# Longer rows for q, k and the weights, and an earlier first block, in a fused attention and feed-forward kernel

## The chip, the cores and the metric

One core of one Trainium2 chip. The metric is the time of one execution on the device, in microseconds; lower is better. The kernel before takes 399.72 us (median of 3 runs, 399.69 to 401.94). A profiled execution's span, from first to last instruction, is about 2 us shorter than its time.

## The reference, cut to what matters

```python
# q, k, v: (8 batches, 8 heads, 576 positions, 64), s: (8, 8, 576)
scores = q @ k.T / 8
cum = cumsum(max(s, 0))                       # a decay along the sequence
bias = min(-(cum[query] - cum[key]), 0)       # causal positions only
attn = softmax(where(causal, -1e9, scores + bias))
x = (attn @ v)        # -> (4608 tokens, 512)
h = x @ w_in          # 512 -> 2048
g = h * clip(h + 3, 0, 6) / 6
return g @ w_out      # 2048 -> 512
```

The kernel works on 32 pairs of heads (four pairs are a batch of 576 tokens) and nine blocks of 512 tokens. "Layer 1" of a block is h and g, "layer 2" is the product with w_out.

## The kernel before: the parts that the argument touches

Loads of a pair, with `NTR` = 9 tiles of 128 rows. Every contiguous piece is one row of 64 fp32 numbers, 256 bytes:

```python
    def load_qk(p, eng):
        t = work.tile([128, NTR, 2, D], F32, tag="qkf", bufs=3, name=f"qkf{p}")
        for i, src in enumerate((q, k)):
            eng.dma_start(
                out=t[:, :, i, :],
                in_=src[b, h0:h0 + 2].rearrange("h s d -> (h s) d").rearrange(
                    "(t p) d -> p t d", p=128
                ),
            )
```

The cast to fp16 on GpSimd (`cast_qk`) is followed by transposes on TensorE into PSUM, in two groups of five and four tiles, and by copies out of PSUM, one for q (rows 0 to 63) and one for k (64 to 127):

```python
        nc.vector.tensor_copy(out=qT[0:64, sl, c0:c0 + n], in_=pT[0:64, 0:n])
        nc.vector.tensor_copy(out=kT[0:64, sl, c0:c0 + n], in_=pT[64:128, 0:n])
```

Four more rows of kT and qT carry the decay (`kaug`, `qaug`). They are computed once for all heads with the heads on partitions, stored to DRAM, and read back for each pair. The last lines weave the work: attention of batch 0 alone, layer 1 of block 0 beside batch 1, then both layers of consecutive blocks beside a batch each:

```python
    weave(att_of[1], m1_tasks(0))
    for n in range(NBLK - 1):
        att = att_of[n + 2] if n + 2 < B else []
        weave(att, merged(m1_tasks(n + 1), m2_tasks(n)))
```

PSUM is full: two banks "M" (layer 1, early transposes), three "S" (scores), two "O" (attend), one "Y" (layer 2).

The softmax here doesn't subtract the row's maximum and nothing guards it: scores larger than these inputs give would overflow.

## Time and profile before

| kernel before | |
|---|---|
| time, median | 399.7 us |
| span of the profile | 397.3 us |
| first exponential | 16.4 us |
| layer 1 of block 0 starts | 45.0 us |
| layer 1 of block 1 starts ("the landmark") | 85.1 us |
| from one block's start to the next, later | 40.1 us |
| last matmul ends | 393.2 us |

The first 80 us are bound by DMA and the rest by TensorE; the prediction below shows the lines that say so. A group's row reads: line, engine, operation, what it writes and reads, count; busy time and mean duration; idle time of the engine before it and what ended most of that. In the kernel before, the copies out of the transposes are these (groups by form):

```profile
L181 DVE COPY qT<-pT 64x640 f16<-64x640 f16 x32 | 15.2, 476 | 16.4 <-PE pT L171 16.4
L182 DVE COPY kT<-pT 64x640 f16<-64x640 f16 x32 | 15.8, 493 | 0.4
L182 DVE COPY kT<-pT 64x512 f16<-64x512 f16 x32 | 13.6, 426 | 0.4
L181 DVE COPY qT<-pT 64x512 f16<-64x512 f16 x32 | 13.1, 408 | 1.3 <-PE pT L171 1.3
```

About 0.45 us each, 57.7 us of DVE for all 32 pairs, on an engine that is busy for 57% of the span.

### The profile page before, as it was taken

How to read it: one execution, taken by the hardware profiler on the slowest of the kernel's cores; microseconds unless marked ns; L12 is line 12 of the kernel's file. 1: busy time of each engine (PE TensorE's matmuls, PEld its weight loads, DVE VectorE, ACT ScalarE, POOL GpSimd, SP SyncE). 2: the span in 40 equal slices, each digit the busy share in tenths (PEclk: the TensorE clock that was granted, in tenths of full speed). 3: DMA queues.
4: the chain of work that ended last, by engine and by line, in shares of the span. 5: the costliest groups of instructions: out<-in, count | busy, mean ns of one | idle time of the engine just before them, and what ended most of it. 6: DMA issues, size and time to landing. Idle time of an engine off the chain costs nothing.

```text
span 397.3 us, 8194 instructions
## 1 busy us (share of the span) xinstructions
PE 366.4 (92%) x3040; PEld 209.7 (53%) x3040; DVE 227.2 (57%) x417; ACT 210.8 (53%) x406; POOL 140.3 (35%) x333
## 2 busy tenths in 40 slices
PE   7584776899999999999999999999999999999985
PEld 3363443555555555555555555555555544444432
DVE  4574372756666666666666666666665564454511
ACT  6364473755555566666666555555556633443400
POOL 3394825544444444444444444444443200000000
PEclk9999698999999999999999999999999999999999
DMA  9999999955555555554555455455100001010111
GB/s 176 201 213 205 185 208 178 194 108 118 116 118 118 119 117 118 119 117 117 118 118 118 108 126 114 109 126 116 38 28 27 28 26 54 26 53 28 49 58 54
DMA packets 123512, 43.40 MB, mean 109 GB/s; under 512 B 114192, under 2 KB 118672, under 8 KB 123472
## 3 DMA queue, kind: packets, MB, share of 16 engines
q1 hardware_dynamic: 117456, 37.89, 43.9%
q0 software_dynamic: 4224, 4.19, 6.4%
q10 hardware_dynamic: 1792, 0.79, 0.9%
q8 instruction: 24, 0.39, 0.4%
q14 instruction: 16, 0.13, 0.1%
HBM read 37.32 MB, written 9.73 MB: 118 GB/s over the span
## 4 chain that ended last, share of the span: by engine, by line
PE 80%; DMA 10%; POOL 4%; DVE 3%; ACT 2%; issue 1%; SPq 0%; POOLq 0%; ACTq 0%
PE po L335 31%; PE ph L317 29%; PE S L211 8%; DMA qkf<-in_k_dram 7%; PE O L260 6%; PE pT L171 3%; PE pX L285 2%; POOL Pm L224 2%; POOL t L153 1%; DMA kaug_scratch<-kaug 1%; DMA kT<-kaug_scratch 1%; ACT trl L325 1%; ACT Pm L219 1%; DMA s_sb<-in_s_dram 1%; DVE osb L344 1%; DVE gT L326 1%
## 5 line engine op out<-in xcount | busy, mean ns | idle before, releaser
L326 DVE SCALAR_TENSOR_TENSOR gT<-trl,ph 128x512 f16<-128x512 f32 x144 | 98.8, 687 | 114.7 <-ACT trl L325 114.5
L219 ACT ACTIVATE Pm<-S 128x384 f16<-128x384 f32 (+2 forms) x256 | 113.7, 506 | 80.3 <-PE S L211 72.5
L317 PE MATMUL ph<-xT,w_in_sb 128*128 128x512 f16 x576 | 147.4, 381 | 0.0
L335 PE MATMUL po<-w_out_sb,gT 128*128 128x512 f16 x576 | 144.4, 379 | 2.3 <-DVE osb L344 2.3
L325 ACT ACTIVATE trl<-ph,bias 128x512 f32<-128x512 f32 x144 | 99.6, 692 | 82.8 <-PE ph L317 81.0
L224 POOL TENSOR_SCALAR_AFFINE_SELECT Pm<-Pm 128x128 f16<-128x128 f16 (+2 forms) x256 | 78.8, 313 | 154.6 <-ACT Pm L219 144.8
L211 PE MATMUL S<-qT,kT 128*128 128x320 f16 (+4 forms) x448 | 71.4, 265 | 8.0 <-DMA kT<-kaug_scratch 3.0
L335 PEld LDWEIGHTS <-gT 128*128 128x128 f16 x576 | 51.2, 98 | 49.4 <-issue 3.2
L317 PEld LDWEIGHTS <-w_in_sb 128*128 128x128 f16 x576 | 52.2, 98 | 44.5 <-issue 1.1
L211 PEld LDWEIGHTS <-kT 128*128 128x128 f16 x448 | 42.1, 99 | 35.3 <-issue 4.9
L153 POOL CAST t<-qkf 128x1152 f16<-128x1152 f32 x32 | 36.7, 1147 | 21.4 <-DMA qkf<-in_k_dram 21.4
L260 PEld LDWEIGHTS <-Pm 128*128 128x128 f16 x960 | 37.4, 97 | 7.8 <-POOL Pm L224 1.6
L260 PE MATMUL O<-v_h,Pm 128*128 128x65 f16 x960 | 40.8, 193 | 0.5 <-POOL Pm L224 0.5
L171 PE MATMUL pT<-ident,t 128*128 128x128 f16 x288 | 26.8, 222 | 13.5 <-POOL t L153 12.9
L181 DVE COPY qT<-pT 64x640 f16<-64x640 f16 x64 | 28.3, 442 | 17.7 <-PE pT L171 17.6
L171 PEld LDWEIGHTS <-t 128*128 128x128 f16 x288 | 21.1, 99 | 28.1 <-POOL t L153 14.6
L344 DVE TENSOR_SCALAR osb<-po 128x512 f32<-128x512 f32 x36 | 24.8, 690 | 13.8 <-PE po L335 13.2
L182 DVE COPY kT<-pT 64x640 f16<-64x640 f16 x64 | 29.4, 459 | 0.9
L272 DVE TENSOR_TENSOR xs<-O,r 128x640 f16<-128x640 f32 x32 | 26.4, 824 | 1.1
L159 POOL CAST v_h<-v_f 128x640 f16<-128x640 f32 x28 | 20.1, 718 | 0.0
L285 PEld LDWEIGHTS <-xs 128*128 128x128 f16 x160 | 11.8, 99 | 10.9 <-issue 6.2
L293 DVE COPY xT<-pX 128x576 f16<-128x576 f16 x32 | 14.5, 453 | 1.7 <-PE pX L285 1.5
(29 smaller groups left out, 56.6 us busy)
## 6 DMA issues: line engine op xcount, KB each, us to landing
qkf<-in_q_dram SPq DMA_DIRECT2D x32, 288.0 KB
qkf<-in_k_dram SPq DMA_DIRECT2D x32, 288.0 KB
out_dram<-osb SPq DMA_DIRECT2D x36, 256.0 KB
v_f<-in_v_dram SPq DMA_DIRECT2D x62, 128.0 KB
w_in_sb<-in_moe_w_in_dram POOLq DMA_DIRECT2D x4, 512.0 KB, 8.1
w_out_sb<-in_moe_w_out_dram POOLq DMA_DIRECT2D x4, 512.0 KB, 10.1
v_f<-in_v_dram SPq DMA_DIRECT2D x31, 32.0 KB
kT<-kaug_scratch SPq DMA_DIRECT2D x30, 6.8 KB
```

Of the source, the lines that this page charges most:

```text
L153: nc.gpsimd.tensor_copy(out=t, in_=qk_f.pop(p))
L171: nc.tensor.matmul(out=pT[:, (t - t0) * 128:(t - t0 + 1) * 128], lhsT=src[:, t, :, :], rhs=ident, is_transpose=True, start=(t == t0), stop ...
L182: nc.vector.tensor_copy(out=kT[0:64, sl, c0:c0 + n], in_=pT[64:128, 0:n])
L211: nc.tensor.matmul(out=S[:, c:c + hi - lo], lhsT=kT[:, sl, off + 128 * kt:off + 128 * (kt + 1)], rhs=qT[:, sl, off + lo:off + hi], start=( ...
L219: nc.scalar.activation(out=P[:, p0:p0 + n], in_=S[:, 0:n], func=AF.Exp, scale=0.125, bias=0.0)
L224: nc.gpsimd.affine_select(out=view, in_=view, pattern=pattern, compare_op=ALU.is_ge, fill=0.0, base=0, channel_multiplier=-1,)
L260: nc.tensor.matmul(out=O[:, hh, qt * VW:qt * VW + D + 1], lhsT=P[:, c:c + 128], rhs=v_h[:, sl, hh, kt, 0:D + 1], start=(qt == 0), stop=(qt ...
L317: nc.tensor.matmul(out=ph, lhsT=w_in_sb[:, kc, f * 128:(f + 1) * 128], rhs=xT[:, kc, n * 512:(n + 1) * 512], start=(kc == 0), stop=(kc == ...
L325: nc.scalar.activation(out=trl, in_=ph, func=AF.Relu, bias=bias3[:, 0:1], scale=1.0)
L326: nc.vector.scalar_tensor_tensor(out=gT[n][:, f, :], in0=trl, scalar=6.0, in1=ph, op0=ALU.min, op1=ALU.mult)
L335: nc.tensor.matmul(out=po, lhsT=gT[n][:, f, t4 * 128:(t4 + 1) * 128], rhs=w_out_sb[:, f, :], start=(f == 0), stop=(f == NF - 1),)
L344: nc.vector.tensor_scalar_mul(out=osb, in0=po, scalar1=1.0 / 6.0)
```

## The change

The intent is to shorten the DMA-bound stage. For pairs 0 to 7 each partition reads nine consecutive rows of q and of k, 2304 bytes in one piece; the transposes then come out with neighbouring rows in different tiles, and the copies out of PSUM put them back in order. The weights are read in 8 KB rows, so that layer 1 takes every sixteenth column of w_in. The decay rows of pair 0 go from SBUF to SBUF. Casts of v move from DVE to ScalarE (pairs 1 to 4), casts of q and k move later, and layer 1 and half of layer 2 of block 0 stand beside batch 1. Three output tiles take an "M" bank. Smaller moves are cut from the diff below: the weight loads are issued one pair earlier, the transposes of the next pair stand ahead of an attend, and the warm-up matmuls are 18 and 12 instead of 22 and 10.

```diff
     def load_qk(p, eng):
...
+            rows = src[b, h0:h0 + 2].rearrange("h s d -> (h s) d")
+            if by_partition(p):                     # p < 8
+                eng.dma_start(
+                    out=t.rearrange("p (i t d) -> p i t d", i=2, d=D)[:, i],
+                    in_=rows.rearrange("(p t) d -> p t d", t=NTR),
+                )
...
     def cast_v(p):
-        eng = nc.vector if p in (1, 2, 3, 4) else nc.gpsimd
-        eng.tensor_copy(out=v_h[:, sl, :, :, 0:D], in_=v_f[:, sl])
+        copy = nc.scalar.copy if p in (1, 2, 3, 4) else nc.gpsimd.tensor_copy
+        copy(out=v_h[:, sl, :, :, 0:D], in_=v_f[:, sl])
...
-        nc.vector.tensor_copy(out=qT[0:64, sl, c0:c0 + n], in_=pT[0:64, 0:n])
-        nc.vector.tensor_copy(out=kT[0:64, sl, c0:c0 + n], in_=pT[64:128, 0:n])
+        for dst, r0 in ((qT, 0), (kT, 64)):
+            if by_partition(p):
+                nc.vector.tensor_copy(
+                    out=dst[0:64, sl, 0:W2].rearrange("d (p t) -> d t p", t=NTR)[:, t0:t1],
+                    in_=pT[r0:r0 + 64, 0:n].rearrange("d (t p) -> d t p", p=128),
+                )
...
     def load_w_in(c):
         nc.gpsimd.dma_start(
-            out=w_in_sb[:, :, c * 512:(c + 1) * 512],
-            in_=moe_w_in[:, c * 512:(c + 1) * 512].rearrange("(kc p) f -> p kc f", p=128),
+            out=w_in_sb[:, c, :], in_=moe_w_in[c * 128:(c + 1) * 128, :]
         )
     def load_w_out(c):
-            in_=moe_w_out[c * 512:(c + 1) * 512, :].rearrange("(ft p) j -> p ft j", p=128),
+            in_=moe_w_out.rearrange("(p f) j -> p f j", f=NF)[:, c * 4:(c + 1) * 4, :],
+    w_in_t = w_in_sb.rearrange("p k (m f) -> p k f m", f=NF)
...
-                lhsT=w_in_sb[:, kc, f * 128:(f + 1) * 128],
+                lhsT=w_in_t[:, kc, f, :],
...
+    load_qk(0, nc.sync)
+    load_qk(1, nc.sync)
+    mask_rows(0, nc.scalar.copy)
+    nc.scalar.activation(out=qaug, in_=c8, func=AF.Copy, scale=-1.0)
+    for hh in range(2):
+        nc.sync.dma_start(out=kT[64:65, 0, c0:c1], in_=kaug[hh:hh + 1, 0, :])
+        nc.scalar.dma_start(out=qT[67:68, 0, c0:c1], in_=qaug[hh:hh + 1, :])
+    for hh in range(2):
+        nc.sync.dma_start(out=kT[65:66, 0, c0:c1], in_=kaug[hh:hh + 1, 1, :])
+        nc.scalar.dma_start(out=kT[66:67, 0, c0:c1], in_=kaug[hh:hh + 1, 2, :])
+    load_v(0, nc.sync)
+    nc.sync.dma_start(out=kaug_dram..., in_=kaug)
+    nc.sync.dma_start(out=qaug_dram..., in_=qaug)
...
-    weave(att_of[1], m1_tasks(0))
+    weave(att_of[1], first + m2_0[:8])              # first: layer 1 of block 0
+    weave(att_of[2], merged(m1_tasks(1), m2_0[8:], 2))
```

More of the change, by code (lines that the diff above doesn't have):

```diff
@@ L118, with by_partition @@
     qk_h = {}
+    def by_partition(p):
+        return p < 8
     def load_qk(p, eng):
         b, h0 = (2 * p) // H, (2 * p) % H
-        t = work.tile([128, NTR, 2, D], F32, tag="qkf", bufs=3, name=f"qkf{p}")
+        t = work.tile([128, NTR * 2 * D], F32, tag="qkf", bufs=3, name=f"qkf{p}")
         for i, src in enumerate((q, k)):
-            eng.dma_start(
-                out=t[:, :, i, :],
-                in_=src[b, h0:h0 + 2].rearrange("h s d -> (h s) d").rearrange(
-                    "(t p) d -> p t d", p=128
-                ),
-            )
+            rows = src[b, h0:h0 + 2].rearrange("h s d -> (h s) d")
[4 more added lines that the diff above has]
+                )
+            else:
+                eng.dma_start(
+                    out=t.rearrange("p (t i d) -> p t i d", i=2, d=D)[:, :, i, :],
+                    in_=rows.rearrange("(t p) d -> p t d", p=128),
+                )
         qk_f[p] = t
@@ L152, in cast_qk @@
         t = work.tile([128, NTR, 2, D], F16, tag="qkh", bufs=2)
-        nc.gpsimd.tensor_copy(out=t, in_=qk_f.pop(p))
+        f = qk_f.pop(p)
+        if by_partition(p):
+            nc.gpsimd.tensor_copy(
+                out=t.rearrange("p t i d -> p i t d"),
+                in_=f.rearrange("p (i t d) -> p i t d", i=2, d=D),
+            )
+        else:
+            nc.gpsimd.tensor_copy(
+                out=t, in_=f.rearrange("p (t i d) -> p t i d", i=2, d=D)
+            )
         qk_h[p] = t
@@ L180, in transpose_group @@
         c0 = t0 * 128
-        nc.vector.tensor_copy(out=qT[0:64, sl, c0:c0 + n], in_=pT[0:64, 0:n])
-        nc.vector.tensor_copy(out=kT[0:64, sl, c0:c0 + n], in_=pT[64:128, 0:n])
+        for dst, r0 in ((qT, 0), (kT, 64)):
+            if by_partition(p):
+                nc.vector.tensor_copy(
+                    out=dst[0:64, sl, 0:W2].rearrange("d (p t) -> d t p", t=NTR)[:, t0:t1],
+                    in_=pT[r0:r0 + 64, 0:n].rearrange("d (t p) -> d t p", p=128),
+                )
+            else:
+                nc.vector.tensor_copy(out=dst[0:64, sl, c0:c0 + n], in_=pT[r0:r0 + 64, 0:n])
         if g == 1:
@@ L331, in m2 @@
         if part == 0:
-            pouts[n, t4] = psum.tile([128, 512], F32, tag="Y", bufs=1, name=f"po{n}_{t4}")
+            tag, bufs = ("M", 2) if (n, t4) in ((0, 1), (8, 1), (8, 3)) else ("Y", 1)
+            pouts[n, t4] = psum.tile([128, 512], F32, tag=tag, bufs=bufs, name=f"po{n}_{t4}")
         po = pouts[n, t4]
@@ L349 @@
     nc.vector.memset(bias3, 3.0)
-    load_qk(0, nc.sync)
-    load_v(0, nc.scalar)
-    load_qk(1, nc.sync)
-    load_v(1, nc.sync)
-    load_qk(2, nc.sync)
-    load_v(2, nc.sync)
-    mask_rows(0, nc.scalar.copy)
-    nc.scalar.activation(out=qaug, in_=c8, func=AF.Copy, scale=-1.0)
-    mask_rows(1, nc.scalar.copy)
-    nc.scalar.dma_start(
-        out=kaug_dram.rearrange("r (h t) -> h r t", h=NH), in_=kaug
-    )
-    nc.scalar.dma_start(out=qaug_dram.rearrange("r (h t) -> h (r t)", h=NH), in_=qaug)
-    load_aug(0, nc.scalar)
-    load_aug(1, nc.scalar)
     def keep_warm(n):
@@ L374, in keep_warm @@
             )
-    weights = {
-        1: [(load_w_in, 0)],
-        2: [(load_w_in, 1), (load_w_in, 2)],
-        3: [(load_w_in, 3)],
-        4: [(load_w_out, 0), (load_w_out, 1)],
-        5: [(load_w_out, 2), (load_w_out, 3)],
+    load_qk(0, nc.sync)
[3 more added lines that the diff above has]
+    for hh in range(2):
+        c0, c1 = hh * SEQ, (hh + 1) * SEQ
+        nc.sync.dma_start(out=kT[64:65, 0, c0:c1], in_=kaug[hh:hh + 1, 0, :])
+        nc.scalar.dma_start(out=qT[67:68, 0, c0:c1], in_=qaug[hh:hh + 1, :])
+    for hh in range(2):
+        c0, c1 = hh * SEQ, (hh + 1) * SEQ
+        nc.sync.dma_start(out=kT[65:66, 0, c0:c1], in_=kaug[hh:hh + 1, 1, :])
+        nc.scalar.dma_start(out=kT[66:67, 0, c0:c1], in_=kaug[hh:hh + 1, 2, :])
+    load_v(0, nc.sync)
+    nc.sync.dma_start(
+        out=kaug_dram.rearrange("r (h t) -> h r t", h=NH), in_=kaug
+    )
+    nc.sync.dma_start(out=qaug_dram.rearrange("r (h t) -> h (r t)", h=NH), in_=qaug)
+    mask_rows(1, nc.scalar.copy)
+    load_v(1, nc.sync)
+    load_qk(2, nc.sync)
+    load_aug(1, nc.sync)
+    load_v(2, nc.sync)
+    weights_at = {
+        0: [(load_w_in, 0)],
+        1: [(load_w_in, 1), (load_w_in, 2)],
+        2: [(load_w_in, 3)],
+        3: [(load_w_out, 0), (load_w_out, 1)],
+        4: [(load_w_out, 2), (load_w_out, 3)],
     }
     def att_tasks(p):
+        more = p + 1 < NP
         def loads():
@@ L392, in loads @@
                 load_v(p + 3, nc.sync)
-            for load, c in weights.get(p, []):
-                load(c)
-        more = p + 1 < NP
-        tasks = [(loads, 0)]
-        for bi in range(4):
-            tasks.append((lambda bi=bi: scores_bank(2 * p, bi), 400))
-        if p > 0:
-            tasks.append((lambda: attend(2 * p - 1), 1200))
-        if more:
-            tasks.append((lambda: transpose_group(p + 1, 0), 640))
-        for bi in range(4):
-            tasks.append((lambda bi=bi: scores_bank(2 * p + 1, bi), 400))
+            if p >= 4 and more:
+                cast_qk(p + 1)
         def casts():
@@ L409, in casts @@
                 cast_v(p + 1)
-            if p + 2 < NP:
+            if p + 2 <= 4:
                 cast_qk(p + 2)
-        tasks.append((casts, 0))
+            for load, c in weights_at.get(p, []):
+                load(c)
+        a = [(loads, 0)]
+        for bi in range(4):
+            a.append((lambda bi=bi: scores_bank(2 * p, bi), 400))
+        if more:
+            a.append((lambda: transpose_group(p + 1, 0), 640))
         if p > 0:
-            tasks.append((lambda: x_transpose(p - 1), 640))
+            a.append((lambda: attend(2 * p - 1), 1200))
+        for bi in range(4):
+            a.append((lambda bi=bi: scores_bank(2 * p + 1, bi), 400))
+        a.append((casts, 0))
         if more:
-            tasks.append((lambda: transpose_group(p + 1, 1), 512))
-        tasks.append((lambda: attend(2 * p), 1200))
-        return tasks
+            a.append((lambda: transpose_group(p + 1, 1), 512))
+        if p > 0:
+            a.append((lambda: x_transpose(p - 1), 640))
+        return a, [(lambda: attend(2 * p), 1200)]
+    att_of = [[]]
+    for p in range(NP):
+        a, c = att_tasks(p)
+        att_of[-1] += a
+        if p % 4 == 0 and p > 0:
+            att_of.append([])
+        att_of[-1] += c
+    att_of[-1] += [(lambda: attend(NH - 1), 1200), (lambda: x_transpose(NP - 1), 640)]
     def weave(att, mlp):
         total = float(sum(c for _, c in att)) or 1.0
-        done = 0.0
-        for i, task in enumerate(mlp):
-            while att and done / total < i / len(mlp):
+        whole = float(sum(w for _, w in mlp))
+        done, due = 0.0, 0.0
+        for task, w in mlp:
+            while att and done / total < due / whole:
                 a, c = att.pop(0)
@@ L430, in weave @@
             task()
+            due += w
         for a, c in att:
@@ L434, in m1_tasks, with merged @@
     def m1_tasks(n):
-        return [lambda f=f: m1(n, f) for f in range(NF)]
+        return [(lambda f=f: m1(n, f), 1.0) for f in range(NF)]
     def m2_tasks(n):
-        return [lambda t4=t4, part=part: m2(n, t4, part) for t4 in range(4) for part in range(4)]
-    def merged(a, b):
-        out_ = []
-        for t in range(4):
-            f, g = a[4 * t:4 * t + 4], b[4 * t:4 * t + 4]
-            out_ += [g[0], g[1], f[0], g[2], f[1], g[3], f[2], f[3]]
+        return [
+            (lambda t4=t4, part=part: m2(n, t4, part), 1.0)
+            for t4 in range(4) for part in range(4)
+        ]
+    def merged(a, b, rounds):
+        out_ = []
+        na = len(a) // rounds
+        for t in range(rounds):
+            f, g = a[na * t:na * (t + 1)], b[4 * t:4 * t + 4]
+            if na == 4:
+                out_ += [g[0], g[1], f[0], g[2], f[1], g[3], f[2], f[3]]
+            else:
+                out_ += [g[0], f[0], f[1], g[1], f[2], f[3], g[2], f[4], g[3]] + f[5:]
         return out_
-    keep_warm(22)
+    keep_warm(18)
     cast_qk(0)
@@ L454 @@
     cast_qk(1)
-    keep_warm(10)
-    att_all = []
-    cut = []
-    for b in range(B):
-        for p in range(4 * b, 4 * b + 4):
-            att_all += att_tasks(p)
-            if p % 4 == 0:
-                cut.append(len(att_all) - 2)
-    att_all += [(lambda: attend(NH - 1), 1200), (lambda: x_transpose(NP - 1), 640)]
-    cut.append(len(att_all))
-    att_of = [att_all[cut[b]:cut[b + 1]] for b in range(B)]
-    for task, _ in att_all[:cut[1]]:
-        task()
-    weave(att_of[1], m1_tasks(0))
-    for n in range(NBLK - 1):
-        att = att_of[n + 2] if n + 2 < B else []
-        weave(att, merged(m1_tasks(n + 1), m2_tasks(n)))
-    for task in m2_tasks(NBLK - 1):
+    keep_warm(12)
+    for task, _ in att_of[0]:
+        task()
+    first = m1_tasks(0)
+    first = [(task, 0.3) for task, _ in first[:8]] + [(task, 0.6) for task, _ in first[8:]]
+    m2_0 = m2_tasks(0)
+    weave(att_of[1], first + m2_0[:8])
+    weave(att_of[2], merged(m1_tasks(1), m2_0[8:], 2))
+    for n in range(2, NBLK):
+        weave(
+            att_of[n + 1] if n + 1 < B else [], merged(m1_tasks(n), m2_tasks(n - 1), 4)
+        )
+    for task, _ in m2_tasks(NBLK - 1):
         task()
```

## The prediction

> **What bounds the kernel now.** I read the slices of the page first, to see where the span is not full.
>
> ```profile
> PE   7584776899999999999999999999999999999985
> PEclk9999698999999999999999999999999999999999
> DMA  9999999955555555554555455455100001010111
> ```
>
> One slice is 9.93 us. From slice 8 on (about 80 us) TensorE is full; before that it is not, and the DMA engines are. So there are two stages: DMA bounds the first 80 us, TensorE the rest. The table of stretches says the same in numbers (length, then busy time and count of PE, PEld, DVE, ACT and POOL, then granted clock, DMA share, GB/s):
>
> ```profile
> 0.00:10.00 10.00, 7.29 (x31) 3.01 (x31) 4.51 (x8) 6.37 (x6) 3.49 (x11) 1.00 1.00 176
> 30.00:40.00 10.00, 4.51 (x74) 3.66 (x73) 4.70 (x10) 4.63 (x12) 3.77 (x10) 0.95 1.17 206
> 60.00:70.00 10.00, 7.00 (x54) 4.24 (x55) 3.38 (x7) 3.83 (x8) 5.61 (x12) 0.83 0.93 178
> 100.00:200.00 100.00, 100.00 (x900) 59.39 (x899) 63.61 (x121) 60.21 (x120) 42.37 (x100) 1.00 0.54 117
> ```
>
> DMA is saturated at only about 200 GB/s, so its packets are too small. What this does to TensorE is in the list of its waits (total, times, longest):
>
> ```profile
> PE pT L171 <- POOL t L153: 12.9, 4, 6.9
> PE S L211 <- DMA kT<-kaug_scratch: 3.0, 1, 3.0
> PE po L335 <- DVE osb L344: 2.3, 3, 0.8
> ```
>
> and behind the first of them, in the chain that ended last (start, length), stand two landings of k:
>
> ```profile
> 12.41 3.57 DMA kT<-kaug_scratch
> ...
> 29.03 11.91 DMA qkf<-in_k_dram
> ...
> 45.22 16.20 DMA qkf<-in_k_dram
> ```
>
> So: the first scores wait for the decay rows' trip through DRAM; then the cast of a later pair, on an in-order GpSimd, waits for its q and k, and everything behind it stops (6.9 and 4.7 us). After both stops the clock drops to half for 6.8 and 3.4 us.
>
> **The dense part as a yardstick.** From the start-to-start spacing of matmuls between 100 and 260 us: 215.8 ns for 512 columns; the seven of a score head sum to 0.69 us; 31.3 ns each for the 15 of attend; 56 ns a transpose. A pair costs 2 x 0.69 + 2 x 0.47 + 14 x 0.056 = 3.1 us, a layer of a block 64 x 0.2158 = 13.8 us. Four pairs and two layers give 40.0 us; the first-layer starts of consecutive blocks are 40.1 us apart, so the late stage has no slack at all. What the change can win lies before a landmark, the first matmul of layer 1 of block 1, and in the tail:
>
> ```profile
> 85.05 1.03 PE L317 MATMUL ph<-xT,w_in_sb 128*128 128x512 f16 x4
> ```
>
> ```profile
> 380.75 3.61 PE L335 MATMUL po<-w_out_sb,gT 128*128 128x512 f16 x16 [0.78 <-DVE osb L344]
> 385.15 3.61 PE L335 MATMUL po<-w_out_sb,gT 128*128 128x512 f16 x16 [0.78 <-DVE osb L344]
> 389.55 3.61 PE L335 MATMUL po<-w_out_sb,gT 128*128 128x512 f16 x16 [0.78 <-DVE osb L344]
> ```
>
> The span ends 4.1 us after the last matmul's 393.2.
>
> **What the Trainium skill says.** "DMA: Bandwidth & Descriptors", section "Specifications": transfers need at least 512 B for line rate. The trace agrees: in its record of each DMA packet a 256-byte packet of q, k or v takes 21.3 ns in the mean (12 GB/s per engine), a 2304-byte packet of s 93 ns (25 GB/s). "VectorE: DVE Perf Modes", section "What auto-detection actually checks": two 16-bit elements a cycle need step one in every tensor. The trace agrees for the copies out of PSUM: 64x640 takes 493 ns and 64x512 426 ns (row kT of the groups by form), so 128 elements cost 67 ns, two per cycle of the stated 0.96 GHz. "SBUF — State Buffer", section "Door 1: The DMA port swizzle": each access that crosses to a new 16-byte line pays a penalty. This bears on w_in, whose weight loads will now step 32 bytes; no run here shows it yet. "TensorE: Matmul & The Clock Gate", section "What's actually happening": an idle window of some 3.4 us halves the clock; the 0.83 above, after a stop, agrees.
>
> **Part by part.**
> (1) q and k of pairs 0 to 7 in rows of 2304 bytes. Before: 2304 packets of 256 bytes for a pair's q and k, /16 engines x 21.3 ns = 3.1 us. After: 256 packets x 93 ns / 16 = 1.5 us. v stays at 1.5 us. A pair falls from 4.6 to 3.0 us; eight pairs save 13 us of DMA time.
> (2) Weights with 8 KB source rows. The page gives their queue 6.4% of the span, 25 us, at 96 ns for 2 KB read; at the 307 ns in which 8 KB packets of the instruction queue pass it would be 20 us. I count 0 to 5 us saved.
> So through pair 7 the DMA work is 8 x 3.0 + 20..25 + about 3 for s, masks and decay rows = 47 to 52 us, where it was 65.
> (3) The price: the DVE copies out of the transposes write with a step of nine. At one element a cycle they take about 0.82 (640) and 0.68 us (512): 3.0 us a pair for 1.8, on DVE, for pairs 0 to 7. The casts of v for pairs 1 to 4 go from DVE (0.55) to ACT (about 0.72, scaled from its 1152-element copy of 1.15).
> (4) Decay rows of pair 0 go SBUF to SBUF. Before, the store was issued at 8.1 and its read landed at 16.0. Now the last row can be issued at about 9 (it waits for the last DVE step at 8.1, for k of pair 1, and for an earlier row) and lands near 11.5. DVE's four strided copies of pair 0 end at 8.1 + 3.0 = 11.1, and the second mask copy keeps ACT till 12.2. So the first exponential starts near 12.2, where it was at 16.4.
> (5) Batch 0 has ten heads of scores before the weave of batch 1 starts. ACT needs 2.03 us for a head's four exponentials plus 0.36 for half a cast of v; 10 x 2.4 = 24 us, with DVE at 4.5 and GpSimd at 4 to 5 us a pair close by. I take 24.5: the weave starts at 36.7, and w_in should have landed by 35 (last chunk issued near 26, landing 8 to 10 us later).
> (6) Batch 1 then holds four pairs, a layer and half a layer: 12.4 + 13.8 + 6.9 = 33.1 us of TensorE. DVE needs 4 x 4.5 + 16 x 0.69 + 1.4 = 30.4 us of that, DMA needs pair 7 by about 50 us, when some 50 us of DMA work stand ahead of it. It is balanced rather than free, so I add 3 us of stalls. The landmark: 36.7 + 33.1 + 3 = 73 us.
> (7) From the landmark on everything is as before, minus six of the eight quarter-tiles of layer 2 that were still ahead at the old landmark (two were done): 6 x 0.86 = 5.2 us. The last block's four outputs now alternate between two PSUM tags, so the three waits of 0.78 go: 2.3 us.
>
> Sum: 73 + (393.2 - 85.1 - 5.2 - 2.3) + 4.1 = 377.7 us of span. The measured time is 1.7 to 2.4 us above the span (399.0 and 399.7 beside 397.3), hence **about 379 us**, a gain of 21 us or 5%.
>
> **Rivals.**
> (a) The strided weight loads of w_in show. A load is 98 ns beside a matmul of 216 ns, and attend gets a load and a matmul through in 31 ns, so even four times that hides. Against: the skill's line penalty[...]. If layer 1 slowed by 10%, 576 x 22 ns = 12.4 us come back: 391 us. I give it 1 in 10.
> (b) DVE becomes the bound of the first 70 us. If the step of nine costs more than one element a cycle (half that rate: 5.4 us a pair instead of 3.0), each of eight pairs loses up to 2 us: 391 us at worst, some 386 with the part that hides. 1 in 7.
> (c) DMA stays the bound: v still comes in 256-byte packets, every pair takes seven issues of 0.25 to 0.6 us on SP[...], and the rows of pair 1 hold SP until the DRAM trip is over. Then batch 1 waits as before but for less: up to 7 us more, 386 us.
> (d) Better than thought: no stalls in batch 1 and batch 0 at its old 2.2 us a head: 372 us.
>
> **Range and chances.** The gains of (4), (7) and of the half layer moved forward (5 us) are nearly sure, 11 us together, over 2% already. The other 10 depend on batch 0 and 1 keeping pace. Rivals (b) and (c) are likelier in part than (d), so the range leans up: 371 to 388. Faster by over 2% (below 391.7): 0.93; within 2%: 0.05; slower: 0.02.
>
> **What would show it.** Right: 2304-byte packets near 93 ns; first exponential at 11.5 to 13; no wait of TensorE on the GpSimd cast above 2 us; clock 1.00 from 15 us on; the landmark at 70 to 76; DMA falling to half share before 65 us; strided copies at 0.8 and 0.7 us; no osb wait in the tail. Wrong: layer 1 spacing above 220 ns (a); strided copies over 1.2 us, with ACT waiting for scores (b); waits on landings of q, k or v over 4 us in all (c); or batch 0 taking more than 28 us from its first exponential.

## The result

**456.48 us** (median of 4 runs, 455.13 to 457.14) where the kernel before took 399.71 us in the same rounds: 14% slower, ratio 1.1406 with a 95% interval of 1.1353 to 1.1458. Ratios here and below are the mean time of one kernel's runs over that of the other's runs of the same rounds, so not quite the ratio of the medians. Executions over 1.5% slower than the fastest of the same kernel are left out of the means.

The slices of the changed kernel's page (40 of 11.4 us), which answer to those of the kernel before at the head of the prediction:

```profile
PE   5623535467659999999999999999999999999996
DVE  6989888867885668665566656656666655544531
PEclk9666665588699999999999999999999999999999
DMA  4677535522144764565644455665440100101111
```

TensorE is full only from slice 12 on, about 136 us, where it had been full from 80 us. DMA is no longer full before that, but mostly because the same loads are spread over a longer stage: from the shares of its queues, DMA work fell only from 205 to 189 us. The busiest engine of the stage is DVE, at 0.8 to 0.9 in most slices.

The stretches (length; busy time and count of PE, PEld, DVE, ACT, POOL; clock; DMA share; GB/s) put numbers to it:

```profile
10.00:20.00 10.00, 4.90 (x15) 1.82 (x16) 9.91 (x5) 2.20 (x2) 1.82 (x2) 0.66 0.73 178
50.00:60.00 10.00, 1.97 (x25) 1.59 (x24) 9.88 (x7) 1.68 (x4) 2.75 (x6) 0.65 0.62 142
200.00:300.00 100.00, 100.00 (x897) 65.89 (x895) 63.99 (x120) 59.91 (x120) 42.38 (x100) 1.00 0.54 117
```

In the first two of these stretches, the fullest of the stage, DVE is busy for 9.9 of 10 us with five or seven instructions; in the others up to 90 us it is busy for 6.2 to 9.2. The groups by form say which instructions these are:

```profile
L202 DVE COPY qT<-pT 64x640 f16<-64x640 f16 x8 | 23.8, 2981 | 8.3 <-PE pT L190 8.3
L202 DVE COPY kT<-pT 64x640 f16<-64x640 f16 x8 | 23.7, 2958 | 0.1
...
L202 DVE COPY qT<-pT 64x512 f16<-64x512 f16 x8 | 19.3, 2410 | 0.0
L202 DVE COPY kT<-pT 64x512 f16<-64x512 f16 x8 | 19.2, 2394 | 0.1
```

A strided copy takes 2.97 us where the contiguous one took 0.48, and 2.40 where it took 0.42. From 512 to 640 elements it grows by 0.57 us, 4.45 ns an element. The 32 of them take 86.0 us; eight pairs of contiguous copies would take 14.4 us (57.7 x 8/32), so DVE has 71.6 us more to do, all of it in the first eight pairs. The chain that ended last shows these copies on the path (start, length):

```profile
21.29 2.99 DVE qT L202
24.30 2.95 DVE kT L202
27.26 2.38 DVE qT L202
29.66 2.40 DVE kT L202
34.19 2.98 DVE qT L202
```

From 21.29 to 34.19, from one pair to the next, there are four copies of 10.7 us and one gap of 2.1 us. TensorE's first wait is now for them, no longer for the cast (total, times, longest):

```profile
PE S L236 <- DVE kT L202: 31.8, 8, 8.8
PE pX L310 <- DVE xs L297: 14.9, 4, 4.9
```

In these gaps the clock record drops to half for 78 us of the first 149 us, where before it had dropped for 10 us of the first 85.

The landmark comes at 149.5 us where it was 85.1, 64.4 us later. Behind it the two kernels match: 301.4 us to the last matmul (450.98 - 149.54) where the kernel before needs 308.1, less by the seven quarter-tiles of layer 2 already done (6.0 us) and the three waits of the tail (2.3 us), more by about 1.6 us, which the experiments below place. So the whole loss lies before the landmark.

### The profile page after: what moved, and what is told of

Read it like the earlier page. It is cut to its first block, busy times and chain, and to the rows that moved or that the text cites. A ratio compares the mean times of both kernels' runs of the same rounds, so it can differ in the third digit from the quotient of the medians.

```text
span 454.7 us, 8197 instructions
## 1 busy us (share of the span) xinstructions
PE 384.6 (85%) x3038; PEld 242.1 (53%) x3038; DVE 298.3 (66%) x413; ACT 213.9 (47%) x410; POOL 139.0 (31%) x333
## 3 DMA queue, kind: packets, MB, share of 16 engines
q1 hardware_dynamic: 102696, 38.49, 36.1%
## 4 chain that ended last, share of the span: by engine, by line
PE 72%; DVE 23%; ACT 2%; issue 1%; DMA 1%; ACTq 0%
PE po L364 27%; PE ph L344 26%; DVE kT L202 9%; PE S L236 9%; DVE qT L202 8%; PE O L285 5%; PE pT L190 3%; PE pX L310 2%; DVE gT L353 2%; ACT Pm L244 1%; DVE xs L297 1%; PE pw L384 1%; ACT trl L352 1%; DMA s_sb<-in_s_dram 1%; DVE osb L373 0%
## 5 line engine op out<-in xcount | busy, mean ns | idle before, releaser
L344 PE MATMUL ph<-xT,w_in_sb 128*128 128x512 f16 x576 | 153.9, 394 | 9.4 <-DVE gT L353 5.6
L344 PEld LDWEIGHTS <-w_in_sb 128*128 128x128 f16 x576 | 77.4, 147 | 37.8 <-issue 11.1
L364 PEld LDWEIGHTS <-gT 128*128 128x128 f16 x576 | 53.5, 98 | 49.1 <-issue 0.6
L202 DVE COPY qT<-pT 64x640 f16<-64x640 f16 (+1 forms) x16 | 43.1, 2695 | 8.3 <-PE pT L190 8.3
L285 PEld LDWEIGHTS <-Pm 128*128 128x128 f16 x960 | 40.9, 103 | 11.9 <-issue 5.1
L285 PE MATMUL O<-v_h,Pm 128*128 128x65 f16 x960 | 44.0, 200 | 0.0
L202 DVE COPY kT<-pT 64x640 f16<-64x640 f16 (+1 forms) x16 | 42.8, 2676 | 0.2
L190 PEld LDWEIGHTS <-t 128*128 128x128 f16 x288 | 22.6, 102 | 18.1 <-issue 7.5
L190 PE MATMUL pT<-ident,t 128*128 128x128 f16 x288 | 28.2, 229 | 1.3 <-POOL t L165 0.7
L310 PE MATMUL pX<-ident,xs 128*128 128x128 f16 x160 | 15.2, 230 | 15.1 <-DVE xs L297 14.9
L170 POOL CAST t<-qkf 128x1152 f16<-128x1152 f32 x24 | 27.6, 1150 | 0.0
L207 DVE COPY qT<-pT 64x640 f16<-64x640 f16 (+1 forms) x48 | 21.4, 445 | 5.7 <-PE pT L190 5.1
```

The lines of the kernel that those rows point to most:

```text
L190: nc.tensor.matmul(out=pT[:, (t - t0) * 128:(t - t0 + 1) * 128], lhsT=src[:, t, :, :], rhs=ident, is_transpose=True, start=(t == t0), stop ...
L202: nc.vector.tensor_copy(out=dst[0:64, sl, 0:W2].rearrange("d (p t) -> d t p", t=NTR)[:, t0:t1], in_=pT[r0:r0 + 64, 0:n].rearrange("d (t p) ...
L285: nc.tensor.matmul(out=O[:, hh, qt * VW:qt * VW + D + 1], lhsT=P[:, c:c + 128], rhs=v_h[:, sl, hh, kt, 0:D + 1], start=(qt == 0), stop=(qt ...
L310: nc.tensor.matmul(out=pX[:, qt * 128:(qt + 1) * 128], lhsT=xs[:, qt, :, :], rhs=ident, is_transpose=True, start=(qt == 0), stop=(qt == 4),)
L344: nc.tensor.matmul(out=ph, lhsT=w_in_t[:, kc, f, :], rhs=xT[:, kc, n * 512:(n + 1) * 512], start=(kc == 0), stop=(kc == KC - 1),)
L364: nc.tensor.matmul(out=po, lhsT=gT[n][:, f, t4 * 128:(t4 + 1) * 128], rhs=w_out_sb[:, f, :], start=(f == 0), stop=(f == NF - 1),)
```

## The experiments

Theory A: the write step of nine fp16 elements makes the copies slow, and that is the whole loss. Rival B: the copies are slow through their read from PSUM or through what runs beside them. Rival C: other parts of the change, the schedule or the strided weight loads, cost time themselves. A second question follows once A holds: does the rest of the change bring what the prediction said?

### probe: copies with different steps, alone

The kernel before, with copies added behind its last instruction, when nothing else runs:

```diff
+    for k in (1, 2, 3, 4, 6, 8, 9, 16):
+        nc.vector.tensor_copy(out=stepped(pr, k), in_=src)      # 64x640, PSUM -> SBUF, write step k
+    nc.vector.tensor_copy(out=stepped(pr, 9), in_=psb[0:64, 0:640])   # the same from SBUF
+    nc.vector.tensor_copy(out=stepped(pr4, 3), in_=src)         # into fp32
+    nc.vector.tensor_copy(out=runs, in_=by_t)                   # runs of five, pitch nine
+    nc.scalar.copy(out=stepped(pr, 9), in_=src)                 # and more of the kind
```

> The kernel before with 16 copies of 64 x 640 elements put behind its last instruction, each alone on its engine: DVE from PSUM with a write step of 1, 2, 3, 4, 6, 8, 9 and 16 fp16 elements; then step 9 from SBUF; step 3 into fp32; the same 640 elements walked so that runs of five neighbours are written at a pitch of nine (and of five); ScalarE with step 1, step 9 and the runs; GpSimd with step 9. Theory A (the step of the write is what costs): step 1 takes 0.49 us, step 9 takes 2.98 us as in the changed kernel, from SBUF too, the small steps lie between, 8, 9 and 16 are alike, and the runs of five are well under 1.5 us. Rival B (the cost is in the read from PSUM, or comes from what runs beside it in the changed kernel): step 9 alone is under 1.2 us, or step 9 from SBUF is, and the runs with their strided PSUM read are slow. For ScalarE I have no expectation beyond 0.65 us at step 1.

Measured. The timeline of the eight DVE copies, in the order of the steps 1, 2, 3, 4, 6, 8, 9, 16 (start, length, what):

```profile
397.13 0.47 DVE L493 COPY xT<-probe_ps 64x640 f16<-64x640 f16 x1
397.64 0.86 DVE L493 COPY xT<-probe_ps 64x640 f16<-64x640 f16 x1
398.54 1.21 DVE L493 COPY xT<-probe_ps 64x640 f16<-64x640 f16 x1
399.78 1.56 DVE L493 COPY xT<-probe_ps 64x640 f16<-64x640 f16 x1
401.38 2.27 DVE L493 COPY xT<-probe_ps 64x640 f16<-64x640 f16 x1
403.69 2.98 DVE L493 COPY xT<-probe_ps 64x640 f16<-64x640 f16 x1
406.70 2.94 DVE L493 COPY xT<-probe_ps 64x640 f16<-64x640 f16 x1
409.67 2.82 DVE L493 COPY xT<-probe_ps 64x640 f16<-64x640 f16 x1
```

The time grows by 0.35 to 0.39 us for each unit of step up to eight elements, which is 16 bytes, and then stays. Step nine alone on the engine takes 2.94 us, as in the changed kernel, so what runs beside it plays no part. The other copies, in the groups by form (L494 DVE step 9 from SBUF, L495 fp32 step 3, L498 runs of five at a pitch of nine, L501 ScalarE step 9, L502 ScalarE runs of five, L503 GpSimd step 9):

```profile
L503 POOL COPY xT<-w_out_sb 64x640 f16<-64x640 f16 x1 | 3.0, 2966 | 101.2 <-ACT xT L502 101.2
L501 ACT COPY xT<-probe_ps 64x640 f16<-64x640 f16 x1 | 2.9, 2943 | 0.0
L494 DVE COPY xT<-w_out_sb 64x640 f16<-64x640 f16 x1 | 1.6, 1557 | 0.0
L495 DVE CAST v_f<-probe_ps 64x640 f32<-64x640 f16 x1 | 1.2, 1214 | 0.0
...
L498 DVE COPY xT<-probe_ps 64x640 f16<-64x640 f16 x1 | 0.8, 799 | 0.0
L502 ACT COPY xT<-probe_ps 64x640 f16<-64x640 f16 x1 | 0.7, 747 | 0.0
```

ScalarE out of PSUM and GpSimd out of SBUF take 2.9 us too, where ScalarE took 0.69 us at step one (on GpSimd no step-one copy was timed): moving the copy to another engine would not help. From SBUF the same write takes half, 1.56 us, which Theory A did not expect; rival B's threshold of 1.2 us was not met either, so a part of the cost depends on the source. And 640 elements into the same kind of place cost 0.80 us if five neighbours are written in a row, with PSUM read at a step of 128 elements. Theory A holds in the main, and the last line is a remedy.

### rows_only and rows_old: the long rows alone, and all but the long rows

`rows_only` is the kernel before with the long rows of q and k and their strided copies; `rows_old` is the changed kernel without them:

```diff
     def by_partition(p):
-        return p < 8
+        return False                                # rows_old
```

> The kernel before with one thing added: q and k of pairs 0 to 7 in rows of 2304 bytes, and the strided copies this needs. Theory A: DVE needs 10.7 us for the copies of a pair, the first eight pairs take about 13 us each, and the time is 450 to 465 us, as slow as the whole change. Rival C: under 425 us, the rest of the loss being in the other parts.

Measured: **463.93 us** (4 runs), ratio to the kernel before of those rounds 1.1572 (1.1538 to 1.1606). This one part by itself makes the kernel slower than the whole change does. Its copies take 2.96 to 2.97 us and 2.38 to 2.39 us.

> The changed kernel with one thing undone: q and k of all pairs in rows of 256 bytes and contiguous copies, as before. Theory A (the strided copies are the whole loss): DVE loses 71 us of work, no stretch is DVE-bound, and the time is 385 to 395 us, below the kernel before because the early scores, the half layer and the tail stay. Rival C (the new schedule, the later casts, or the strided loads of w_in cost time themselves): the time stays above 405 us.

Measured: **399.3 us** (396.09 to 401.93, 4 runs), ratio 0.9978 (0.9896 to 1.0059): the same as the kernel before. Without the long rows nothing is lost, so rival C falls as a cause of the loss; but the 385 to 395 us that I expected are missed too. The four times stand in two groups, 396.1 and 396.7, and 401.9 twice; no run explains the gap. The rest of the change brings next to nothing while q and k come in 256-byte rows: TensorE again waits for the cast and the cast for q and k:

```profile
PE pT L190 <- POOL t L170: 13.0, 6, 6.3
```

### runs: the same copies walked in another order

The changed kernel with the two inner dimensions of the copy exchanged. Same elements, same places:

```diff
-                    out=dst[0:64, sl, 0:W2].rearrange("d (p t) -> d t p", t=NTR)[:, t0:t1],
-                    in_=pT[r0:r0 + 64, 0:n].rearrange("d (t p) -> d t p", p=128),
+                    out=dst[0:64, sl, 0:W2].rearrange("d (p t) -> d p t", t=NTR)[:, :, t0:t1],
+                    in_=pT[r0:r0 + 64, 0:n].rearrange("d (t p) -> d p t", p=128),
```

> The changed kernel with the two inner loops of the strided copies exchanged: the same elements go to the same places, but five (or four) neighbours are written one after the other and PSUM is read with a step of 128 elements. Theory A: elements that follow each other within a few bytes are cheap, the copies take 0.8 to 1.5 us, and the time is 378 to 395 us. Rival B (the order does not matter, or the strided read of PSUM costs as much): the copies stay above 2.2 us and the time above 440 us.

Measured: **394.22 us** (392.26 to 394.81, 4 runs), ratio to the kernel before 0.9826 (0.9789 to 0.9863). One exchange of two dimensions takes back 62 us. The copies, by form:

```profile
L202 DVE COPY kT<-pT 64x640 f16<-64x640 f16 x8 | 6.6, 827 | 0.1
L202 DVE COPY qT<-pT 64x640 f16<-64x640 f16 x8 | 6.5, 815 | 12.9 <-PE pT L190 12.9
L202 DVE COPY kT<-pT 64x512 f16<-64x512 f16 x8 | 5.8, 726 | 0.1
L202 DVE COPY qT<-pT 64x512 f16<-64x512 f16 x8 | 5.7, 714 | 0.2 <-PE pT L190 0.2
```

This is the cost that the prediction had put down, 0.82 and 0.68 us. So `runs` is also the kernel that the prediction described, and it lets the rest of its sum be tested: 379 us was predicted, 394 us came. Term by term, from the profile of `runs`:

| | predicted | runs |
|---|---|---|
| first exponential | 12.2 us | 13.6 us |
| from there to layer 1 of block 0 (batch 0) | 24.5 us | 32.5 us |
| from there to the landmark (batch 1) | 36.1 us | 41.8 us |
| landmark | 73 us | 87.9 us |
| landmark to the last matmul | 300.6 us | 301.4 us |

One part of the answer stands in this profile already. With the copies mended the DMA engines are full again from 20 to 60 us (shares 1.02, 1.08, 0.89 and 1.12 in steps of 10 us), and the chain that ended last goes through two landings, the second of them until 40.3 us:

```profile
20.10 7.60 DMA v_f<-in_v_dram
29.64 10.66 DMA qkf<-in_k_dram
```

Within batch 0 the casts wait 6.4 us for landings (GpSimd 4.1 us for k, ScalarE 2.3 us for v). The next five runs ask what else makes batch 0 and batch 1 longer.

### runs_nov: less DMA work

```diff
-                load_v(p + 3, nc.sync)
+                if p + 3 > 7:
+                    load_v(p + 3, nc.sync)          # wrong output on purpose
```

> The version with runs of five and four (394.2 us), and v of pairs 3 to 7 not loaded at all (the output is wrong on purpose; the casts read the slots as they are). About 7 us of DMA work fall out of the first 60 us. Theory D (with the copies mended, DMA still sets the pace of the first 60 us, because v comes in 256-byte packets and because the DMA engines stood half idle in the first 20 us): the landmark, 87.9 us, comes 5 to 8 us sooner and the time is 386 to 390 us. Rival E (the in-order queues or the halved clock pace it, not the transfers): the landmark moves by less than 2 us, the time stays above 392 us.

Measured: 391.36 us (390.38 to 392.43), ratio 0.9767 (0.9728 to 0.9806); the output is wrong, as meant. In its profile batch 0 took 27.2 us (32.5 in `runs`), batch 1 took 41.8 us in both. So the loads of v have no part in batch 1's length. For batch 0 they have some, but less than the two profiles suggest: each is one execution, that of `runs` is its slowest and stood at half clock for 10 us around 40 us, and the two runs that follow, with all of v loaded, show 28.2 and 27.6 us. The times say 2.9 us (394.22 to 391.36), with intervals that overlap a little. Theory D expected more, and the landmark moved by 3.8 us, between the two.

### runs_order: the sync queue in another order

```diff
     load_qk(1, nc.sync)
+    load_v(0, nc.sync)
+    load_qk(2, nc.sync)
     mask_rows(0, nc.scalar.copy)
... (and removed from their places behind the decay rows)
```

The reason is in the first two stretches of `runs`:

```profile
0.00:10.00 10.00, 7.35 (x27) 2.84 (x27) 6.08 (x9) 4.16 (x4) 2.99 (x10) 1.00 0.48 152
10.00:20.00 10.00, 6.62 (x57) 3.92 (x57) 5.89 (x9) 7.40 (x14) 5.44 (x12) 1.00 0.77 183
```

The DMA engines, full in the kernel before (1.00 and 1.02), are half and three quarters busy: the sync queue issues in order and stands at the decay rows, which wait for DVE (2.6 us in the list of its waits).

> The version with runs of five and four, and on the sync queue v of pair 0 and q and k of pair 2 issued before the decay rows of pair 0 rather than behind them, so that the DMA engines have work while that queue waits for the rows. Theory D: the DMA share of the first 20 us rises by 2 to 3 us of work, the rows come at most 1 us later, and the time falls by 2 to 4 us, to 390 to 392 us. Rival E: no change, or slower by the later rows (394 to 396 us).

Measured: 394.02 us (391.81 to 396.25), ratio 0.9848 (0.9788 to 0.9908): no change that these runs resolve. The share rose to 0.79 in the first 10 us and fell to 0.46 in the next; 1.25 of 2.00 in the sum became 1.25. The queue only stood still a little later. The expectation of 2 to 4 us was wrong.

### runs_oldaug: the start of the kernel before

The start, up to the loads of pair 2, is replaced by that of the kernel before, decay rows through DRAM included.

> The version with runs of five and four, and the start of the kernel before put back: v of pair 0 on the scalar queue, v and q and k of pairs 1 and 2 issued at once, the decay rows of pair 0 through DRAM. The first exponential goes back from 13.6 us to about 16. If the early rows are worth what they moved, the time rises by 2.5 to 3 us, to about 397 us. If Theory D holds, the DMA engines are full from the start here, and the later first scores cost little or nothing: 391 to 395 us.

Measured: 392.76 us (392.35 to 393.24), ratio 0.9798 (0.977 to 0.9827). The first exponential came at 16.6 us, 3.0 later than in `runs` (1.4 to 3.2 later than in the four profiles with that start, where it came at 13.4 to 15.2), and layer 1 of block 0 at 44.2 us, 1.9 *earlier*. The decay rows from SBUF to SBUF are worth nothing that these runs show: what they bring forward is waited for again in batch 0, where the casts of `runs` wait 6.4 us for landings and those of this run not at all.

### runs_win and runs_nohalf: the strided weights and the half layer

```diff
-                lhsT=w_in_t[:, kc, f, :],
+                lhsT=w_in_sb[:, kc, f * 128:(f + 1) * 128],   # runs_win: wrong output on purpose
```

> The version with runs of five and four, and layer 1 reading 128 adjacent columns of w_in instead of every sixteenth (the output is wrong on purpose, since w_out stays in the other order). If the strided weight loads are hidden, loads fall from 146 to 98 ns and the time stays within 1 us of 394.2; the dense block period, 40.3 us, may fall to the 40.1 of the kernel before, worth 1.6 us. If they delay matmuls, the time falls by more than 3 us.

Measured: 391.66 us (390.5 to 393.26), ratio 0.9773 (0.9732 to 0.9815). Weight loads fell from 146 to 98 ns, as two rows of groups show, `runs` first:

```profile
L344 PEld LDWEIGHTS <-w_in_sb 128*128 128x128 f16 x576 | 76.9, 146 | 32.1 <-issue 4.3
```

```profile
L344 PEld LDWEIGHTS <-w_in_sb 128*128 128x128 f16 x576 | 52.0, 98 | 48.7 <-issue 4.2
```

The starts of consecutive blocks are 39.8 to 40.0 us apart, in `runs` 40.1 to 40.3; from the third block to the seventh 159.7 us (123.3 to 283.0) where `runs` took 160.9 (123.4 to 284.3), so 1.2 us there, and over all blocks from the landmark to the last matmul 300.0 us instead of 301.4. Nearly all of the 48 ns is hidden behind matmuls of 216 ns. The rest of the 2.6 us in the time is within the spread of these runs.

```diff
-    weave(att_of[1], first + m2_0[:8])
-    weave(att_of[2], merged(m1_tasks(1), m2_0[8:], 2))
+    weave(att_of[1], first)                              # runs_nohalf
+    weave(att_of[2], merged(m1_tasks(1), m2_0, 4))
```

> The version with runs of five and four, and the half layer of block 0 put back beside batch 2. Batch 1 then holds 28 us of TensorE work where it held 34 us in 41.8 us. If batch 1 is paced by TensorE, or by the PSUM banks that layer 1 waits for, it gets 5 to 7 us shorter, the half layer is paid later, and the time stays within 2 us of 394.2. If batch 1 is paced by DMA, it stays near 41 us and the time rises by 5 to 6 us, to about 400 us.

Measured: 397.72 us over all four runs; one of them (403.39) was slow, and the three fast ones took 395.72 to 398.74. The ratio of the fast ones is 0.9956 (0.9908 to 1.0004), where `runs` has 0.9826 in its own rounds: by the times the half layer is worth about 1.3%, 5 us. The profiles give less. Batch 1 shrank by 3.0 us (38.8 for 41.8) when 6 us of matmuls left it, and the stretch behind the landmark grew by 5.2 us (306.6 for 301.4), so 2.2 us in all; most of the rest lies in batch 0 (34.3 us for 32.5), which the half layer does not touch. So its worth is 2 to 5 us. Batch 1 lies between the two expectations: it has idle time that the half layer fills in part.

Where that idle time is can be read from the run with the new order, between 43.2 and 84.9 us. I took the matmul spacings of the dense stage as the work (34.4 us) and the rest as lost (7.3 us); 4.8 us of it stand ahead of layer 1. TensorE's waits in this stretch name the cause as far as the profile does:

```profile
PE ph L344 <- DVE gT L353: 2.3, 4, 1.0
PE ph L344 <- DVE xT L318: 0.7, 1, 0.7
```

Layer 1 has two banks, and DVE, busy with copies and the softmax's division in between, frees them late. That is argued, not shown: `best_act` below takes copies off DVE, and batch 1 does not get shorter. What is shown is that batch 1 took 41.7 to 41.8 us in all seven profiles with mended copies that have the half layer and all copies on DVE, with or without v, with either start, order and column layout; none of these sets its length.

### best_order, best_oldaug, best_act: is there a faster version?

All three have runs of five and four, the long rows, and weights with adjacent columns (w_in in 8 KB rows, w_out in 2 KB rows as before). `best_order` adds the new order of the sync queue, `best_oldaug` the old start, and `best_act` is `best_order` with one more edit:

```diff
+                copy = nc.scalar.copy if (dst is kT and p >= 5) else nc.vector.tensor_copy
```

> Runs of five and four, v of pair 0 and q and k of pair 2 issued ahead of the decay rows, and weights whose columns lie side by side: w_in still in 8 KB rows, layer 1 reading 128 adjacent columns, w_out in 2 KB rows as in the kernel before. The output is right. Dense block period 40.0 us where it was 40.3 us, over seven periods 2.3 us; w_out costs DMA at most 2 us more. I expect 390 to 392 us.

> The same with the start of the kernel before (decay rows of pair 0 through DRAM) instead of the new order. If the start does not matter, as the run with that start said (392.8 beside 394.2), this is as fast as the one in the new order: 389 to 392 us.

> The version with the new order and adjacent columns, and the copies of k out of the transposes of pairs 5 to 7 on ScalarE (0.75 us for 640 elements) instead of DVE (0.82 us). Batch 1 lost 7 us of TensorE time in the run with the new order, mostly where layer 1 waits for a PSUM bank that DVE has yet to free. If DVE's queue is what holds the banks, batch 1 falls from 41.7 to about 39 us and the time by 2 to 3 us; if ScalarE becomes the holder instead, no gain or a loss of 1 to 2 us.

Measured, with the kernel before at 398.37 us in these rounds: `best_order` 392.49 us (ratio 0.9824, 0.9775 to 0.9873); `best_oldaug` **391.37 us** (0.9811, 0.9782 to 0.9841); `best_act` 393.98 us (0.9871, 0.9828 to 0.9914). Only `best_oldaug` came within its expected range; `best_order` missed its own by half a microsecond. With the copies on ScalarE batch 1 was 43.2 us long, for 41.8 in `best_order`: no gain. `best_oldaug`, `best_order`, `runs` and `runs_oldaug` cannot be told apart by their intervals; each beats both kernels, the kernel before by 1.7 to 2.0%.

### probe2: the rule behind the copies

> The kernel before with 11 DVE copies behind its end, each alone. fp32 destination from PSUM, 240 elements, steps 1, 2, 3, 4, 8; fp16 destination, 240 elements, steps 1 and 9; fp16 step 9 from SBUF with 639 elements (odd); contiguous fp16 writes of 640 elements read from SBUF with step 9, and with step 1; 640 elements in runs of two at a pitch of nine. Theory L (the cost is one unit of 4.4 ns for each new 16-byte line that a 2-byte write moves to, and never under one element a cycle): fp16 step 9 takes 0.13 + 240 x 0.0044 = 1.19 us; runs of two at a pitch of 18 bytes touch 320 to 360 lines and take 1.5 to 1.7 us, half of single elements; the odd count from SBUF goes back from 1.56 to 2.9 us if two ports had shared the lines; reads with a step are free (0.8 us or less). For fp32 the first probe had 1.21 us at step 3 where the rule gives 2.24: if the unit is 32 bytes for it, 240 elements take about 0.38 us at steps 1 and 2, 0.53 at 3, 0.66 at 4 and 1.19 at 8; if fp32 costs half a unit per line, step 8 stays near 0.66. Rival (every write with a step pays per element, whatever its neighbours): runs of two take 2.9 us.

Measured, each alone. Step 9 in fp16 with 240 elements took 1196 ns, as the rule says (0.13 + 240 x 0.0044). Runs of two at the pitch of nine took 1.31 us for 640 elements, less than half of single elements, so the rival is out. But it is also less than the 1.5 to 1.7 us that the rule gave, so the rule of one fixed cost for each new line is not exact either:

```profile
L499 DVE COPY xT<-w_out_sb 64x639 f16<-64x639 f16 x1 | 1.6, 1556 | 0.0
...
L503 DVE COPY xT<-probe_ps 64x640 f16<-64x640 f16 x1 | 1.3, 1314 | 0.0
L500 DVE COPY xT<-w_out_sb 64x640 f16<-64x640 f16 x1 | 0.7, 742 | 0.0
...
L501 DVE COPY xT<-w_out_sb 64x640 f16<-64x640 f16 x1 | 0.3, 318 | 0.0
```

L500 reads with a step of nine and writes contiguously: 0.74 us, about 1.0 ns an element when the fixed 0.13 us is taken off, so a strided read from SBUF is cheap and a strided write is not. L501 is contiguous on both sides. The odd count from SBUF (L499) still takes half of the cost from PSUM, so an even split over two ports was not the reason, or an odd count does not prevent it; this test cannot tell the two apart, and the reason stays open. fp32 at steps 1, 2, 3, 4, 8 took 390, 401, 467, 569 and 578 ns for 240 elements: flat from 16 bytes on as well, at (578 - 130) / 240 = 1.9 ns an element, less than half of fp16's 4.4. I have no rule that gives both.

## Why the prediction was wrong

**The step that failed is (3): "The DVE copies out of the transposes write with a step of nine. At one element a cycle they take about 0.82 (640) and 0.68 us (512)".** They took 2.97 and 2.40 us, 10.7 us a pair where 3.0 was written. The unit was not one cycle an element but 4.4 ns, 4.3 cycles of the 0.96 GHz that the prediction used; the probe shows this cost for every step of 16 bytes or more. 7.7 us more for each of eight pairs is 62 us, on a serial path of transposes, copies, scores and exponentials; the time came out 77 us above the prediction, and `runs`, where the copies cost what was written, came out 15 us above it. So the copies account for 62 us of the error and other steps for 15.

Two of my own sentences should have stopped me. The Trainium skill, "SBUF — State Buffer", section "Door 1: The DMA port swizzle", was cited for the cost of crossing to a new 16-byte line, and applied to the strided weight loads alone; the copies write 18 bytes apart. The sentence on step one, from "VectorE: DVE Perf Modes", was shortened too far: that section gives step one as the condition of one of two modes with two elements a cycle; the other needs source and destination in SBUF. For copies out of PSUM the prediction's reading stands, but it says only that the fast mode is lost, not what the slow one costs at a step of nine. And rival (b), DVE as the bound, was right as a mechanism but sized at twice the cost at worst (391 us, 1 in 7; a slower kernel had a chance of 0.02) with no row of the profile behind the factor: no copy of the kernel before writes with such a step, so the trace had no duration for it. A cost with no row deserves a range as wide as the ignorance.

**(1), (2): right in the sum, less so in the terms.** In `runs`, all packets up to the landing of q and k of pair 7, at 56.0 us, took 48.8 us of the 16 engines, where 47 to 52 us by about 50 us were predicted. The weight queue took 4.9% of the 454.7 us in the changed kernel, 22 us, within the 20 to 25. But the q and k packets took 105 ns in the mean in `runs` (93 in the median), 1.7 us a pair and not 1.5: the prediction had set the median of all 2304-byte packets, which it called the time of those of s (139 ns in the mean), beside the mean of the small ones. Its 307 ns for 8 KB was the shortest such packet; the weights' took 344 in the mean. In the changed kernel DMA stopped being the bound because DVE had become it; with the copies mended it bounds much of batch 0 again.

**(4): mis-sized, and without effect.** The first exponential came at 13.6 us in `runs`, for 12.2 (13.4 to 15.2 in the four profiles with this start). With the old start it came 3.0 us later and the kernel was not slower (392.76 for 394.22). The early rows were counted as sure; they are off the path as long as batch 0 waits for data.

**(5): mis-sized by 8 us in `runs`.** Batch 0 took 32.5 us, not 24.5. Over the nine profiles with mended copies its length goes with one wait inside it, that of GpSimd's cast for k to land. Without such a wait batch 0 took 27.2 (v left out), 27.3 and 27.6 us (old start); with 3.6 us of it 28.2 (new order), with 4.1 us 32.5 (`runs`), and with 5.4 to 8.4 us 30.9 to 34.3 (the other four). So rival (c), DMA, came true by the sign that the prediction had given for it, waits on landings of over 4 us (6.4 in `runs`, with v), and some 5 of the 8 us go with it. The other 3 us stand in the profiles without these waits too, and no run says what they are. This is read from one profile of each kernel: by the times, leaving v out is worth 3 us, and `runs_order`, meant to fill the first 20 us in which the in-order sync queue left the DMA engines part idle (0.48 and 0.77), gained nothing. The clock stood at half for at most 6.8 us before the landmark where batch 0 took up to 28.2 us, and for 10.2 to 17.1 us in the others; whether that adds to the waits or only follows them, no run separates.

**(6): mis-sized by 5.7 us.** 34.4 us of matmuls, predicted 33.1, plus 7 us of waits, predicted 3. Taking v out did not shorten it, so the loads of v are no cause; 4.8 of the 7.3 us stand ahead of layer 1, where 2.3 us of waits for its PSUM banks are named, and the rest was not separated.

**(7): right.** 300.6 us predicted from the landmark to the last matmul, 301.4 found in the changed kernel and in `runs`. Seven quarter-tiles were done ahead, not six, which the strided weight loads gave back. The waits of the tail are gone. The half layer, put at 5 us, is worth 2 to 5.

**Rival (a) was rightly held small.** Weight loads rose from 98 to 147 ns and the median spacing of matmuls stayed 216 ns; the cost is about 1.5 us in all.

## What to carry to other kernels

When a DMA is made longer by letting a partition read neighbouring rows, the permutation has to be undone somewhere; find that instruction and price it from a probe before anything else, with the very steps that it will have. Walk such a copy so that the innermost dimension writes neighbours and put the step on the read side: the same 640 fp16 elements took 0.80 us that way and 2.94 us the other way. And a stage that stops being bound by one engine is bound by the next: with the copies mended the whole change was worth 1.7 to 2%, not the 5% of the sum, in which batch 0 and batch 1 had been given too little time.

## What the Trainium skill lacked or had wrong

- "SBUF — State Buffer", section "Door 1: The DMA port swizzle", says that 16-bit data can stride by up to 8 elements for free. For 2-byte writes out of PSUM step 2 already took 0.86 us where step 1 took 0.47, and the cost rose by 0.35 us per unit to 2.98 us at step 8, flat from there (64x640). The 16-byte line is borne out as the place where it levels off; "free up to 8" is not, for writes out of PSUM.
- "VectorE: DVE Perf Modes", section "Mode 1× (REGULAR) — the baseline", gives one result a cycle and counts odd strides among what works in this mode. With a write step of nine fp16 elements DVE gave one in 4.45 ns out of PSUM, 4.3 cycles; with a *read* step of nine from SBUF and contiguous writes 640 elements took 0.74 us, which is about one a cycle.
- No page gives the cost of such a write on ScalarE or GpSimd: 2.94 us (from PSUM) and 2.97 us (from SBUF) for 640 elements, beside DVE's 2.94 from PSUM. For GpSimd a cost of the step is stated for reads alone.
- No page gives the cost of such writes in fp32 or of a step of nine from SBUF: 1.9 ns an element in fp32 at 16 bytes and more, and 1.56 us instead of 2.94 us for the fp16 write of step nine when the source is SBUF. Why the first is less than half of fp16's 4.4 ns is open, and so is the second here.
- "TensorE: Matmul & The Clock Gate", section "Weight-path perf modes — Fast Weight Load (FWL) and DoubleRow", names packed and strided reads in one line and gives no difference in cost. Loads of 128 columns 32 bytes apart took 146 ns where adjacent ones took 98 ns; matmuls of 512 columns hid nearly all of it.
